# Attention split in three, first chunks laid out anew, W by a GpSimd sum and one exponential

The kernel runs on one core of a Trainium2 chip. The metric is device time in microseconds (us), less is better. All times are of executions of the whole program; span is the time from the first to the last instruction in the trace.

## The reference

An mLSTM cell feeds a feed-forward network (FFN) with squared relu; everything is fp32.

```python
# q, k, v, o_gate: (4, 8, 768, 40); i_gate, f_gate: (4, 8, 768); w_in (320, 2048); w_out (2048, 320)
for t in range(S):                                  # per batch and head
    m_new  = maximum(f[t] + m, i[t])
    f_stab = exp(f[t] + m - m_new);  i_stab = exp(i[t] - m_new);  m = m_new
    C = f_stab * C + i_stab * outer(v[t], k[t])
    n = f_stab * n + i_stab * k[t]
    y[t] = sigmoid(o[t]) * (C @ q[t]) / maximum(abs(n @ q[t]), 1)
x = y as (B*S, H*D) = (3072, 320)
out = maximum(x @ w_in, 0) ** 2 @ w_out             # weights arrive as float64 words
```

The kernel computes the cell in 24 chunks of 128 tokens (six for each batch). For a chunk, W is a masked matrix exp(A + b) of 128x1024 (8 heads of 128x128), the scores are weighted with it, and a state C is carried from chunk to chunk. The weights are rounded from float64 words in 26 pieces (10 of w_in, 16 of w_out) by ScalarE (`mag`, `low`) and VectorE (four instructions, `join`). All of w_out must be rounded by the time the second FFN matrix (FFN2) begins, near 122 us. What lies between the first FFN block and FFN2 is called the rounding stage below.

## The kernel before

`...` marks cuts.

```python
        def join(self):                       # rounding, VectorE's part of one piece
            ...                               # max/min, shift, and/xor on VectorE
            nc.vector.tensor_tensor(dst.bitcast(I32), bits, low.bitcast(I32), op=ALU.add)
            self.b.append(None)
            self.fetch()                      # the next weight piece's transfer

    def weigh(s):                             # W of chunk s
        ...
        if len(A) == 1:
            nc.gpsimd.affine_select(A[0][:], A[0][:], ...)      # the mask, 128x1024
        for i in range(len(A)):
            hh = slice(i * n, (i + 1) * n)
            for h in range(n):                                   # one exponential per head, b as bias
                nc.scalar.activation(d["W"][:, i * n + h, :], A[i][:, h, :], AF.Exp, bias=b_T[...])
            nc.scalar.activation(d["dec"][:, hh], A[i][:, :, P - 1], AF.Exp)
        values(s)

    def attend(s):
        # hi = qT * C (3 banks of pool ps_at in turn), dC = k * vw, hp = P * va, then on VectorE:
        # num = hi * eA;  Cn = dC * bdm;  and on GpSimd the update of C
        ...
    # half-steps u = 0..7 of the rounding stage
        else:                                  # u odd
            ...
            attend(s)
            rounding.step()
            normalise(s)                       # num += hp, dm, x_sb: VectorE
            ...
            transposes(s + 1)                  # kT by ScalarE, qT copied by VectorE (L356)
            ...
        while rounding.done < NEXT[u]:
            rounding.step()
```

## Time and profile before

| | before |
|---|---|
| time, median of 3 | 619.71 us (619.48 to 619.84) |
| span of the profiled run, mean granted clock | 618.4 us, 0.967 |
| first FFN block ends / FFN2 begins | 43.56 / 121.77 us |
| from there to the end | 496.6 us, TensorE without a wait but at the very end |
| TensorE at half clock | 10.7-17.5, 27.8-41.4, 68.7-75.6, 82.4-89.2, 109.7-116.5 us: 41.0 us |

The half-clock intervals are read from the clock column of narrow windows (0.50 or 0.51 in each of the five). A half-clock interval is counted as costing at most half its length (16 `hp` matmuls took 3.50 us in one against 1.92 us at full clock), so 41.0 us is 20.5 us of "lost clock", which is also span x (1 - mean granted clock). It is an upper bound, since idle time at half clock is counted too. The clock column has no record of the first 3.9 us. The table of windows of the kernel before, cut where the first FFN block ends and where FFN2 begins (columns: length, busy time of TensorE, its weight loads, VectorE, ScalarE, GpSimd, clock, share of the DMA engines, GB/s):

```profile
0.00:43.56 43.56, 35.93 (x205) 27.96 (x207) 30.25 (x64) 22.45 (x56) 9.83 (x20) 0.76 0.78 158
43.56:121.77 78.21, 66.48 (x414) 55.91 (x411) 58.36 (x127) 51.15 (x113) 9.98 (x11) 0.87 0.82 165
121.77:618.40 496.63, 493.24 (x2240) 310.53 (x2238) 144.42 (x294) 126.98 (x326) 47.80 (x56) 1.00 0.23 46
```

Everything to be won is in the first two rows: only there is TensorE idle, but for 3.4 us at the very end, and only there is the clock under 1.

### The profile page before, as it was taken

The numbers are of one execution on the slowest core, as the hardware profiler recorded it, in microseconds if no ns is written. First come the engines' busy times: TensorE is split into PE (matmuls) and PEld (weight loads), VectorE is DVE, ScalarE is ACT, GpSimd is POOL, SyncE is SP. The second block draws the span as 40 slices with busy tenths as digits, with TensorE's granted clock in tenths as the row PEclk, the third lists the DMA queues.
The fourth block names the chain that finished last, engine by engine and source line by source line (L and its number), as shares of the span: only waits on it lengthen the run. The fifth ranks groups of instructions, "written<-read, shape, count | busy, mean of one in ns | idle before, by whom it ended". The sixth has DMA issues, their size and how long they took to land.

```text
span 618.4 us, 7545 instructions
## 1 busy us (share of the span) xinstructions
PE 595.6 (96%) x2851; PEld 394.4 (64%) x2851; DVE 233.0 (38%) x485; ACT 200.6 (32%) x494; POOL 67.6 (11%) x87
## 2 busy tenths in 40 slices
PE   9688878999999999999999999999999999999997
PEld 6576757877655477745477754577754577743575
DVE  6858847743134341134331243421233441112200
ACT  4384657740514320214321514312214222012100
POOL 3211201021011110101110210000210120000000
PEclk8869779799999999999999999999999999999999
DMA  9927796993321332221331422031301000000000
GB/s 194 202 69 159 158 191 142 187 163 65 77 43 47 63 55 67 71 49 35 61 69 46 88 43 57 11 67 56 76 12 34 1 1 22 12 11 0 1 21 22
DMA packets 130901, 42.47 MB, mean 69 GB/s; under 512 B 101073, under 2 KB 127697, under 8 KB 130865
## 3 DMA queue, kind: packets, MB, share of 16 engines
q1 hardware_dynamic: 130768, 41.79, 33.5%
q8 instruction: 23, 0.38, 0.3%
q10 hardware_dynamic: 96, 0.20, 0.1%
q14 instruction: 14, 0.11, 0.1%
HBM read 37.95 MB, written 4.03 MB: 68 GB/s over the span
## 4 chain that ended last, share of the span: by engine, by line
PE 90%; ACT 4%; DVE 4%; DMA 1%; issue 1%; SPq 0%; DVEq 0%; ACTq 0%
PE o_ps L516 34%; PE h_ps L464 23%; PE h_ps L469 7%; PE hp L404 6%; PE tp L352 4%; PE h_ps L488 4%; PE tp L365 3%; PE hi L390 3%; PE dC L397 3%; PE tp L449 1%; DMA kq<-in_q_dram 1%; ACT W_sb L328 1%; PE A_ps L309 1%; PE h_ps L495 1%; PE A_ps L301 1%
## 5 line engine op out<-in xcount | busy, mean ns | idle before, releaser
L516 PE MATMUL o_ps<-w_out,g 128*128 128x320 f32 x768 | 213.8, 435 | 0.0
L516 PEld LDWEIGHTS o_ps<-w_out,g 128*128 128x128 f32 x768 | 143.5, 190 | 57.9 <-issue 0.8
L464 PE MATMUL h_ps<-xT,w_in 128*128 128x512 f32 x320 | 146.9, 602 | 0.0
L473 DVE TENSOR_TENSOR g<-r_sb 128x512 f32<-128x512 f32 x80 | 51.7, 688 | 148.0 <-ACT r_sb L472 148.0
L464 PEld LDWEIGHTS h_ps<-xT,w_in 128*128 128x128 f32 x320 | 57.7, 190 | 69.9 <-issue 65.2
L472 ACT ACTIVATE r_sb<-h_ps 128x512 f32<-128x512 f32 x80 | 43.5, 595 | 162.6 <-PE h_ps L469 162.5
L522 ACT COPY y_sb<-o_ps 128x320 f32<-128x320 f32 x24 | 10.2, 426 | 184.3 <-PE o_ps L516 184.3
L328 ACT ACTIVATE W_sb<-A_bc,b_T 128x128 f32<-128x128 f32 x176 | 53.7, 392 | 0.0
L379 DVE TENSOR_TENSOR P_sb<-tp,W_sb 128x512 f32<-128x512 f32 x46 | 29.6, 685 | 56.8 <-PE tp L365 45.4
L404 PE MATMUL hp<-va,P_sb 128*128 128x41 f32 x368 | 46.8, 290 | 0.0
L404 PEld LDWEIGHTS hp<-va,P_sb 128*128 128x128 f32 x368 | 45.6, 202 | 0.0
L469 PE MATMUL h_ps<-xT,w_in 64*128 64x512 f32 x160 | 45.2, 641 | 0.0
L356 DVE COPY qT<-tp 128x512 f32<-128x512 f32 x23 | 15.8, 688 | 73.5 <-PE tp L352 73.5
L339 POOL TENSOR_TENSOR vw<-va,W_sb 128x328 f32<-128x328 f32 x20 | 15.0, 751 | 258.7 <-ACT W_sb L328 244.9
L488 PE MATMUL h_ps<-xT,w_in 128*128 128x256 f32 x128 | 37.2, 453 | 5.0 <-ACT xT L450 4.6
L488 PEld LDWEIGHTS h_ps<-xT,w_in 128*128 128x128 f32 x128 | 29.0, 234 | 11.3 <-ACT xT L450 5.2
L423 POOL TENSOR_TENSOR C_sb<-C_sb,Cd 128x328 f32<-128x328 f32 x16 | 14.1, 880 | 163.1 <-DVE C_sb L415 163.1
L469 PEld LDWEIGHTS h_ps<-xT,w_in 64*128 64x128 f32 x160 | 12.0, 184 | 30.3 <-issue 30.3
L365 PEld LDWEIGHTS tp<-qT,kT 40*128 40x128 f32 x384 | 24.1, 187 | 10.1 <-issue 5.9
L352 PE MATMUL tp<-ident,kq 128*128 128x128 f32 x192 | 28.8, 299 | 1.7 <-DMA kq<-in_k_dram 1.2
L390 PEld LDWEIGHTS hi<-C_sb,qT 128*128 128x128 f32 x160 | 20.0, 191 | 12.9 <-issue 11.5
L365 PE MATMUL tp<-qT,kT 40*128 40x128 f32 x384 | 27.1, 280 | 0.9 <-DVE qT L356 0.9
(84 smaller groups left out, 442.6 us busy)
## 6 DMA issues: line engine op xcount, KB each, us to landing
A_bc<-a_rows SPq DMA_DIRECT2D x22, 512.0 KB, 3.9
raw<-in_moe_w_out_dram SPq DMA_DIRECT2D x16, 320.0 KB, 3.1
raw<-in_moe_w_in_dram SPq DMA_DIRECT2D x8, 512.0 KB, 4.8
kq<-in_k_dram SPq DMA_DIRECT2D x24, 160.0 KB, 3.8
kq<-in_q_dram SPq DMA_DIRECT2D x24, 160.0 KB, 4.5
va<-in_v_dram SPq DMA_DIRECT2D x24, 160.0 KB, 4.2
og<-in_o_gate_dram SPq DMA_DIRECT2D x24, 160.0 KB, 4.2
out_dram<-y_sb SPq DMA_DIRECT2D x24, 160.0 KB, 1.8
```

What stands on the lines that cost most here:

```text
L328: nc.scalar.activation(d["W"][:, i * n + h, :], A[i][:, h, :], AF.Exp, bias=b_T[:, b, c, i * n + h : i * n + h + 1],)
L352: nc.tensor.transpose(tp[:, j, :], d["kq"][:, i, 2 * j : 2 * j + 2, :].rearrange("p h d -> p (h d)"), ident[:],)
L365: nc.tensor.matmul(sc[i][:, j, :], lhsT=d["kT"][rows, j, :], rhs=d["qT"][rows, j, :], start=True, stop=True,)
L379: nc.vector.tensor_tensor(t, d["sc"][i], d["W"][:].rearrange("p (j two) t -> p j two t", two=2)[:, :, i, :], op=ALU.mult,)
L390: nc.tensor.matmul(hi[:, 2 * j : 2 * j + 2, :].rearrange("p h d -> p (h d)"), lhsT=d["qT"][:, j, :], rhs=C[:, j].rearrange("p h d -> p (h ...
L404: nc.tensor.matmul(hp[:, h, :], lhsT=d["P"][h % 2][:, h // 2, :], rhs=d["va"][:, h, :], start=True, stop=True,)
L464: nc.tensor.matmul(h[:], lhsT=w_in[:, a, fb * P : (fb + 1) * P], rhs=xT[:, a, :], start=(a == 0), stop=False,)
L469: nc.tensor.matmul(hs[i][:], lhsT=w_in2[rows, p, :], rhs=xT[rows, 2, :], start=False, stop=True)
L472: nc.scalar.activation(r[:], hs[i][:], AF.Relu)
L473: nc.vector.tensor_tensor(st["g2"][:, 2 * p + i, :], r[:], r[:], op=ALU.mult)
L488: nc.tensor.matmul(hs[i][:, n, :], lhsT=w_in[:, a, fb * P : (fb + 1) * P], rhs=xT[:, a, cols], start=(n == 0 and a == 0), stop=False,)
L516: nc.tensor.matmul(o_ps, lhsT=st["g2"][:, fb, j * P : (j + 1) * P], rhs=w_out[:, fb, :], start=(fb == 0), stop=(fb == NF - 1),)
```

## The change

The intent: take the eight exponentials of W off ScalarE (one sum on GpSimd, one exponential of 128x1024), take the last add of three weight pieces off VectorE, split the attention into `history`, `update` and `inside` so that the first two chunks can be laid out with fewer waits, load chunk 3 earlier, and lend PSUM banks otherwise. The diff, cut to its core:

```diff
-            nc.vector.tensor_tensor(dst.bitcast(I32), bits, low.bitcast(I32), op=ALU.add)
+            (nc.gpsimd if n < IN_DONE[0] else nc.vector).tensor_tensor(
+                dst.bitcast(I32), bits, low.bitcast(I32), op=ALU.add,
+            )
...
     def weigh(s):                        # chunks 2 to 23; chunks 0 and 1 keep eight (weigh_half)
+        nc.gpsimd.tensor_tensor(
+            d["W"][:], d["A"][:], b_T[:, b, c, :].unsqueeze(2).to_broadcast([P, H, P]), op=ALU.add,
+        )
+        nc.gpsimd.affine_select(d["W"][:], d["W"][:], ...)
-            for h in range(n):
-                nc.scalar.activation(d["W"][:, i * n + h, :], A[i][:, h, :], AF.Exp, bias=b_T[...])
+        nc.scalar.activation(d["dec"][:], d["A"][:, :, P - 1], AF.Exp)
+        nc.scalar.activation(d["W"][:], d["W"][:], AF.Exp)
...
+    def attend(s):
+        if s % NB:
+            history(s)                   # hi, and num right behind it on VectorE
+        if s % NB + 1 < NB:
+            update(s)                    # dC, Cn, C
+        inside(s)                        # hp
...
     # first chunks (after scores, W and weighted of chunks 0 and 1)
+    do_b(2, NB)                          # earlier: before, behind normalise(1)
+    scores(1)
+    weighted(1, spare=True)
+    turn_gates(2, NB)
     ...
+    update(0)
+    inside(0)
     ...
+    inside(1)
+    normalise(0)
+    history(1)
+    turn_rows(0)
+    normalise(1)
+    update(1)
+    idle(4)                              # bf16 matmuls on zeros, meant to keep the clock
     transposes(2)
+    rounding.join()
+    load_part(3, 0)
+    load_part(3, 1)
     ...
         else:                            # u odd
+            rounding.step()
             ...
             attend(s)
-            rounding.step()
             normalise(s)
```

More of the change, by code (lines that the diff above doesn't have):

```diff
@@ L252, in turn_gates @@
         for src, dst in ((i_sb, b_T), (A_sb, eA_T)):
-            tp = ps_o.tile([P, W], F32, name="tp", tag="o_ps")[:, : (c1 - c0) * BH]
+            tp = ps_h.tile([P, W], F32, name="tp", tag="h_ps") if c0 else ps_o.tile([P, W], F32, name="tp", tag="o_ps")
+            tp = tp[:, : (c1 - c0) * BH]
             tp = tp.rearrange("p (c r) -> p c r", r=BH)
@@ L292, in load_A @@
         A = ld.tile([P, H, P], F32, name="A_bc", bufs=2)
-        d["A"] = [A]
+        d["A"] = A
         nc.sync.dma_start(
@@ L296, in load_A, with mask_A @@
         )
-    def mask_A(s):
-        A = ps_h.tile([P, H // 2, P], F32, name="A_ps", tag="h_ps")
+    def mask_A(s, i):
+        pool, tag = (ps_at, "at") if s and i else (ps_h, "h_ps")
+        A = pool.tile([P, H // 2, P], F32, name="A_ps", tag=tag)
         nc.tensor.matmul(
@@ L312, in spread_A, with weigh_half @@
             )
+    def weigh_half(s, i):
+        b, c = divmod(s, NB)
+        d = st[s]
+        A, n = d["A"][i], H // 2
+        if i == 0:
+            d["W"] = prep.tile([P, H, P], F32, name="W_sb")
+            d["dec"] = prep.tile([P, H], F32, name="dec")
+        for h in range(n):
+            nc.scalar.activation(
+                d["W"][:, i * n + h, :], A[:, h, :], AF.Exp, bias=b_T[:, b, c, i * n + h : i * n + h + 1],
+            )
+        nc.scalar.activation(d["dec"][:, i * n : (i + 1) * n], A[:, :, P - 1], AF.Exp)
+        if i == 1:
+            values(s)
     def weigh(s):
@@ L316, in weigh @@
         d = st[s]
-        A, n = d["A"], H // len(d["A"])
         d["W"] = prep.tile([P, H, P], F32, name="W_sb")
-        d["dec"] = prep.tile([P, H], F32, name="dec")
-        if len(A) == 1:
-            nc.gpsimd.affine_select(
-                A[0][:], A[0][:], compare_op=ALU.is_ge, fill=-1e30, base=0, pattern=[[0, H], [1, P]], channel_multiplier=-1,
-            )
-        for i in range(len(A)):
-            hh = slice(i * n, (i + 1) * n)
-            for h in range(n):
-                nc.scalar.activation(
-                    d["W"][:, i * n + h, :], A[i][:, h, :], AF.Exp, bias=b_T[:, b, c, i * n + h : i * n + h + 1],
-                )
-            nc.scalar.activation(d["dec"][:, hh], A[i][:, :, P - 1], AF.Exp)
+        nc.gpsimd.tensor_tensor(
+            d["W"][:], d["A"][:], b_T[:, b, c, :].unsqueeze(2).to_broadcast([P, H, P]), op=ALU.add,
+        )
+        nc.gpsimd.affine_select(
+            d["W"][:], d["W"][:], compare_op=ALU.is_ge, fill=-1e30, base=0, pattern=[[0, H], [1, P]], channel_multiplier=-1,
+        )
+        d["dec"] = prep.tile([P, H], F32, name="dec")
+        nc.scalar.activation(d["dec"][:], d["A"][:, :, P - 1], AF.Exp)
+        nc.scalar.activation(d["W"][:], d["W"][:], AF.Exp)
         values(s)
@@ L381, in weighted, with history @@
             )
-    def attend(s):
+    def history(s):
+        d, C = st[s], st["C"]
         b, c = divmod(s, NB)
-        d = st[s]
-        C = st.get("C")
-        if c > 0:
-            hi = ps_at.tile([P, H, D1], F32, name="hi", tag="at")
-            for j in range(PR):
-                nc.tensor.matmul(
-                    hi[:, 2 * j : 2 * j + 2, :].rearrange("p h d -> p (h d)"), lhsT=d["qT"][:, j, :],
-                    rhs=C[:, j].rearrange("p h d -> p (h d)"), start=True, stop=True,
-                )
-        if c + 1 < NB:
-            dC = ps_at.tile([P, PR, 2, D1], F32, name="dC", tag="at")
-            for j in range(PR):
-                nc.tensor.matmul(
-                    dC[:, j].rearrange("p h d -> p (h d)"),
-                    lhsT=d["kq"][:, 0, 2 * j : 2 * j + 2, :].rearrange("p h d -> p (h d)"),
-                    rhs=d["vw"][:, 2 * j : 2 * j + 2, :].rearrange("p h d -> p (h d)"), start=True, stop=True,
-                )
+        d["hi"] = hi = ps_at.tile([P, H, D1], F32, name="hi", tag="at")
+        for j in range(PR):
+            nc.tensor.matmul(
+                hi[:, 2 * j : 2 * j + 2, :].rearrange("p h d -> p (h d)"), lhsT=d["qT"][:, j, :],
+                rhs=C[:, j].rearrange("p h d -> p (h d)"), start=True, stop=True,
+            )
+        num = d["num"] = work.tile([P, H, D1], F32, name="num")
+        nc.vector.tensor_tensor(
+            num[:], hi[:], eA_T[:, b, c, :].unsqueeze(2).to_broadcast([P, H, D1]), op=ALU.mult,
+        )
@@ new lines, in update @@
+    def update(s):
+        d, C = st[s], st.get("C")
+        dC = ps_at.tile([P, PR, 2, D1], F32, name="dC", tag="at")
+        for j in range(PR):
+            nc.tensor.matmul(
+                dC[:, j].rearrange("p h d -> p (h d)"),
+                lhsT=d["kq"][:, 0, 2 * j : 2 * j + 2, :].rearrange("p h d -> p (h d)"),
+                rhs=d["vw"][:, 2 * j : 2 * j + 2, :].rearrange("p h d -> p (h d)"), start=True, stop=True,
+            )
+        Cn = work.tile([P, PR, 2, D1], F32, name="C_sb")
+        nc.vector.tensor_tensor(Cn[:], dC[:], bdm[:], op=ALU.mult)
+        if s % NB:
+            Cd = work.tile([P, H, D1], F32, name="Cd")
+            nc.gpsimd.tensor_tensor(
+                Cd[:], C[:].rearrange("p j i d -> p (j i) d"),
+                d["dec"][:].unsqueeze(2).to_broadcast([P, H, D1]), op=ALU.mult,
+            )
+            Cf = Cn[:].rearrange("p j i d -> p (j i) d")
+            nc.gpsimd.tensor_tensor(Cf, Cf, Cd[:], op=ALU.add)
+        st["C"] = Cn
@@ L402, in attend, with inside @@
+    def inside(s):
+        d = st[s]
         hp = d["hp"] = ps_at.tile([P, H, D1], F32, name="hp", tag="at")
@@ L406, in attend @@
             )
-        d["num"] = hp
-        if c > 0:
-            num = d["num"] = work.tile([P, H, D1], F32, name="num")
-            nc.vector.tensor_tensor(
-                num[:], hi[:], eA_T[:, b, c, :].unsqueeze(2).to_broadcast([P, H, D1]), op=ALU.mult,
-            )
-        if c + 1 < NB:
-            Cn = work.tile([P, PR, 2, D1], F32, name="C_sb")
-            nc.vector.tensor_tensor(Cn[:], dC[:], bdm[:], op=ALU.mult)
-            if c > 0:
-                Cd = work.tile([P, H, D1], F32, name="Cd")
-                nc.gpsimd.tensor_tensor(
-                    Cd[:], C[:].rearrange("p j i d -> p (j i) d"),
-                    d["dec"][:].unsqueeze(2).to_broadcast([P, H, D1]), op=ALU.mult,
-                )
-                Cf = Cn[:].rearrange("p j i d -> p (j i) d")
-                nc.gpsimd.tensor_tensor(Cf, Cf, Cd[:], op=ALU.add)
-            st["C"] = Cn
+        d.setdefault("num", hp)
+    def attend(s):
+        if s % NB:
+            history(s)
+        if s % NB + 1 < NB:
+            update(s)
+        inside(s)
     def normalise(s):
@@ L570 @@
     make_consts()
+    load_part(1, 0)
+    load_part(1, 1)
     fetch(1)
-    for i in range(3):
-        load_part(1, i)
+    load_part(1, 2)
     fetch(1)
@@ L576 @@
     load_o(1)
-    fetch(2)
-    idle(7)
-    mask_A(0)
-    mask_A(0)
-    mask_A(1)
+    idle(4)
+    mask_A(0, 0)
+    mask_A(0, 1)
+    mask_A(1, 0)
     transposes(0)
+    mask_A(1, 1)
     do_gates(0, 2)
@@ L588 @@
     scores(0)
-    weigh(0)
+    spread_A(1, 0)
+    weigh_half(0, 0)
+    weigh_half(0, 1)
+    weigh_half(1, 0)
     do_gates(2, NB)
-    nc.scalar.dma_start(A_d[:, :], A_sb[:])
-    rounding.words()
-    spread_A(1, 0)
-    transposes(1, (False, True))
-    mask_A(1)
-    spread_A(1, 1)
-    weighted(0)
-    scores(1, (True, True))
-    weigh(1)
-    rounding.join()
-    load(2)
-    load_A(2)
-    attend(0)
-    weighted(1, spare=True)
-    rounding.words()
-    sigmoid(0)
-    sigmoid(1)
-    normalise(0)
-    load_o(2)
-    load_o(3)
-    rounding.join()
-    attend(1)
-    turn_rows(0)
-    normalise(1)
-    do_b(2, NB)
+    nc.sync.dma_start(A_d[:, :], A_sb[:])
+    fetch(2)
+    load_part(2, 0)
+    load_part(2, 1)
+    load_A(2)
+    load_part(2, 2)
+    weighted(0)
+    transposes(1, (True, True))
+    spread_A(1, 1)
+    weigh_half(1, 1)
+    do_b(2, NB)
+    scores(1)
+    weighted(1, spare=True)
     turn_gates(2, NB)
@@ L619 @@
     rounding.words()
+    update(0)
+    inside(0)
+    sigmoid(0)
+    sigmoid(1)
+    rounding.words()
+    rounding.join()
+    load_o(2)
+    load_o(3)
+    inside(1)
+    normalise(0)
+    st[1].pop("num")
+    history(1)
+    turn_rows(0)
+    normalise(1)
+    update(1)
+    idle(4)
     transposes(2)
+    rounding.join()
+    load_part(3, 0)
+    load_part(3, 1)
     turn_rows(1)
-    rounding.join()
+    rounding.step()
     weigh(2)
@@ L627 @@
     LOAD_A = (3,), (), (4,), (5,), (), (6,), (7,), (8,)
-    LOAD = (3,), (4,), (), (5,), (6,), (7,), (8,), (9,)
+    LOAD = (), (4,), (), (5,), (6,), (7,), (8,), (9,)
     LOAD_O = (), (), (4,), (5,), (6, 7), (), (8, 9), (10, 11)
@@ L631 @@
         s = 2 + u // 2
-        if u == 0:
-            ffn1_half(0, 0, 0)
-            scores(s)
-            rounding.step()
-            weighted(s)
-        elif u % 2 == 0:
-            scores(s)
-            turn_rows(s - 1)
-            ffn1_half(0, u // 4, u % 4)
+        if u % 2 == 0:
+            if u == 0:
+                ffn1_half(0, 0, 0)
+                scores(s)
+            else:
+                scores(s)
+                turn_rows(s - 1)
+                ffn1_half(0, u // 4, u % 4)
             rounding.step()
@@ L643 @@
         else:
+            rounding.step()
             if u in (1, 5):
@@ L647 @@
             attend(s)
-            rounding.step()
             normalise(s)
@@ L654 @@
                 ffn1_half(0, u // 4, u % 4)
+        for r in LOAD_A[u]:
+            load_A(r)
         while rounding.done < NEXT[u]:
             rounding.step()
+        if u == 0:
+            load_part(3, 2)
         square_half()
@@ L659 @@
             weigh(s + 1)
-        for r in LOAD_A[u]:
-            load_A(r)
         for r in LOAD[u]:
```

## The prediction

> **What bounds the kernel now.** First the busy table and the slices of the page.
>
> ```profile
> PE 595.6 (96%) x2851; PEld 394.4 (64%) x2851; DVE 233.0 (38%) x485; ACT 200.6 (32%) x494; POOL 67.6 (11%) x87
> ...
> PE   9688878999999999999999999999999999999997
> ...
> PEclk8869779799999999999999999999999999999999
> ```
>
> TensorE is the bound: 618.4 us less 595.6 busy leaves 22.8 us idle, nearly all in the first eight slices (to 124 us); the clock drops below 9 tenths only there. A mean granted clock of 0.967 means 0.033 x 618.4 = 20.4 us of lost clock time. So some 40 us is all that can be won, and only before 125 us; after that the queue of FFN matmuls never waits, and any us saved early comes off the end. Next, TensorE's waits (us in total, times, longest):
>
> ```profile
> PE hi L390 <- DVE P_sb L379: 5.2, 2, 2.7
> PE tp L256 <- DVE i_sb L249: 4.6, 1, 4.6
> PE h_ps L488 <- ACT xT L450: 4.6, 2, 3.6
> ...
> PE tp L352 <- DMA kq<-in_k_dram: 1.2, 1, 1.2
> ```
>
> The timeline shows what is behind the first and third: the eight exponentials of W.
>
> ```profile
> 62.08 1.28 ACT L328 ACT_TABLE_LOAD   x1
> ...
> 63.37 2.44 ACT L328 ACTIVATE W_sb<-A_bc,b_T 128x128 f32<-128x128 f32 x8
> 65.56 1.29 DVE L379 TENSOR_TENSOR P_sb<-tp,W_sb 128x512 f32<-128x512 f32 x2 [2.08 <-ACT W_sb L328]
> ...
> 66.39 1.09 PE L390 MATMUL hi<-C_sb,qT 128*128 128x82 f32 x8 [2.73 <-DVE P_sb L379]
> ```
>
> TensorE stops 2.73 us there for W of chunk 3, 3.62 us at 80.2 us for a row copy queued behind W of chunk 4 on ScalarE, 2.44 us at 106.3 us for W of chunk 5. Together 8.8 us. Last, GpSimd against VectorE:
>
> ```profile
> 27.86 1.10 POOL L322 TENSOR_SCALAR_AFFINE_SELECT A_bc<-A_bc 128x1024 f32<-128x1024 f32 x1
> 27.98 1.01 DVE L433 TENSOR_TENSOR dm<-dm,num 128x8 f32<-128x8 f32 x1
> ...
> 52.50 0.17 DVE L433 TENSOR_TENSOR dm<-dm,num 128x8 f32<-128x8 f32 x1
> ```
>
> The same tiny VectorE instruction takes 1.01 us while GpSimd works and 0.17 us otherwise.
>
> [...] in half-microsecond windows the clock falls or rises at 10.7, 17.5, 27.8, 41.4, 68.7, 75.5, 82.4, 89.2, 109.7 and 116.5 us[...]. [...]
>
> [...]
>
> [...] The trace has 751 ns for 328 elements[...].
>
> [...] The trace's 671 ns for 512 and 494 ns for 320 elements extend to 1.14 us.
>
> **The change part by part.**
>
> 1. W of chunks 2 to 23. ScalarE loses eight activations (2.44 us a chunk) and gains one of about 1.1 us: 1.3 us saved. GpSimd gains a sum of 1024[...], ahead of the select of 1.1 us that stays (1097 ns in the groups). From 125 us on a chunk takes some 22 us of TensorE time and GpSimd is 11% busy; sum and select end long before ScalarE asks, and the extra blocking of VectorE (33% busy) is hidden. Worth 0 there. Before 125 us it shortens the three waits: 3 x 1.3 = 3.9 us gained.
>
> 2. Loads of chunk 3. Its k and q were issued at 48.2 us, because they stood behind weight fetches that wait for buffers; TensorE waited 1.15, 0.52 and then 0.87 us for the copy of qT. Now they stand before most of those fetches. The copy's 0.7 us stays: 1.8 us gained.
>
> 3. The first two chunks. Before, the last gate transposes waited 4.6 us for two VectorE sums (L248, L249) queued behind the normalising of chunk 1; now the sums come right after qT of chunk 1 and their transposes before the attention products, so that wait goes. But scores of chunk 1 now take a bank in which the mask and gates of chunk 1's second half lay, so TensorE must wait for its four exponentials and `dec` (1.15 + 0.2 us, L328 and L331), some 1.4 us. [...] the clock should drop at 17.5 us, just before the small products of the attention. At half clock a product of 16 such instructions took 3.50 us (hp at 109.64) against 1.92. Two of these, two of dC and one of hi (1.1 us each, doubled on the weight loads) lose 2 x 1.6 + 3 x 0.65 = 5.2 us[...]. Then FFN would begin near 36 us as before, but wait for weight piece 1: VectorE gets to it only after qT of chunk 2, and its last add moves to GpSimd [...]. If the clock holds instead, FFN begins near 31 us. Before, the first FFN block ended at 43.5 us; with the drop I get 44.1, without it 37 to 38. I give the drop 6 in 10: 0.6 x (-0.6) + 0.4 x 6 = 2.0 us gained.
>
> 4. Lost clock. Of the three drops after 60 us each stretches what follows by about 3 us (16 L488 matmuls took 6.35 against 3.62 us after the wait at 83.85). With waits of about 1.3, 2.3 and 1.1 us, one of three should go, perhaps two: 3.5 us gained.
>
> 5. VectorE. Rounding three weight pieces moves 0.69 us each to GpSimd, outside the bottleneck. Against it, between 36 and 122 us VectorE is the second busiest engine (8.5, 7.3, 9.2 of 10 us from 50 to 80)[...]. A rounding step also now stands ahead of the attention's sums. [...]
>
> Sum: 3.9 + 1.8 + 2.0 + 3.5 - 3.1 = 8.1 us gained; 619.7 - 8.1 = 611.6.
>
> **The rivals.** (a) VectorE becomes the bound of the rounding stage. For it: 75% busy there already, strict order, GpSimd locks seen in the trace. Against: before it idled 2 to 3 us at each W wait. Worked through with every lock falling on it, qT of chunk 3 comes 3 us later, TensorE idles, a new clock drop follows, and the gain shrinks to about 2 us: 617.5. (b) The clock holds from 4 us through the prologue and two of the later drops go. [...] Then 6 more in part 3 and 3 in part 4: 602 to 604. (c) The first stage loses the clock already at 10.7 us [...]: the first FFN block ends near 48 us, 4.5 us later than now, and the other parts about pay for it: 616 to 621. (d) Later chunks: the exponential waits on GpSimd in ScalarE's queue and holds up the relus. With 20 us a chunk of slack I see no us in it.
>
> **Range and chances.** Between (a), near 617.5, and (b), near 603, with the sum at 611.6: 602.5 to 618.5. Faster by over 2% means under 607.3 us; only (b) or parts of it reach that: 0.27. Slower by over 2% (632) needs a new regular wait after 125 us, which I don't see: 0.02. The rest, 0.71.
>
> **What would show it.** After 130 us no wait of TensorE and an unchanged matmul rhythm (part 1); an exponential of 128x1024 at 1.0 to 1.2 us [...]; no DMA wait for k of chunk 3 (part 2); no wait at L256's successor, a wait of TensorE on ScalarE near 15 to 16 us and a clock drop at 17.5 us (part 3); at most two drops after 60 us (part 4); VectorE instructions of a microsecond or two beside the GpSimd sums (part 5). I'm wrong if the first FFN block doesn't end between 36 and 46 us, if the sum on GpSimd takes over 3 us, or if TensorE waits after 130 us.

The sum came to 8.1 us gained, 611.6 us. No trace here shows what makes the clock fall or rise; that a shorter wait keeps it (part 4) was the estimate. Measured in the kernel before: 751 ns is GpSimd's product `vw` (L339), 671 and 494 ns are ScalarE's `mag` (L179); "locks" stands for the 0.17 us that became 1.01 us beside a select; and 16 weight loads of `hp` took 1.87 us at full and 3.41 us at half clock.

## The result, and the profile after

| | before | after |
|---|---|---|
| time, median (fast runs) | 619.78 us (619.48 to 620.08, 4 runs) | 620.79 us (619.88 to 622.85, 4 runs) |
| span, clock of the profiled run | 618.4 us, 0.967 | 617.9 us, 0.967 |
| first FFN block ends / FFN2 begins | 43.56 / 121.77 us | 44.57 / 121.88 us |
| half clock | 41.0 us | 11.8-35.7, 49.3-56.2, 83.5-86.9, 110.8-117.6 us: 41.0 us |

The ratio is 1.0021, with a 95% interval of 0.9996 to 1.0046: the same time. A ratio here is the mean time of one kernel's fast runs over that of the other's of the same rounds, so it is not quite the ratio of the medians. The predicted 611.6 us (602.5 to 618.5) is missed on the slow side.

The page of the changed kernel, to be read beside the same lines of before in the prediction:

```profile
PE 598.3 (97%) x2851; PEld 397.2 (64%) x2852; DVE 261.5 (42%) x482; ACT 170.5 (28%) x340; POOL 114.7 (19%) x112
...
PEclk8587989799999999999999999999999999999999
```

ScalarE lost 30.1 us of work, GpSimd gained 47.1 and VectorE 28.5, though three adds had left VectorE. These 28.5 us are not new work but instructions that last longer. The windows, cut at the same two events:

```profile
0.00:44.57 44.57, 40.55 (x205) 32.74 (x208) 28.91 (x60) 18.22 (x44) 12.78 (x21) 0.73 0.79 152
44.57:121.88 77.31, 65.03 (x413) 53.76 (x411) 65.95 (x129) 50.19 (x97) 20.72 (x19) 0.89 0.81 172
121.88:617.90 496.02, 492.70 (x2240) 310.72 (x2238) 166.64 (x294) 102.06 (x200) 81.16 (x73) 1.00 0.23 45
```

The last row: VectorE holds 22 us more there and GpSimd 33 us more, and the stage is not slower (496.0 against 496.6 us). The second row is where the change should have paid. VectorE went from 58.4 of 78.2 us (75%) to 66.0 of 77.3 us (85%), TensorE idles 12.3 us against 11.7, and nothing is won. TensorE's waits of the changed kernel (us in total, times, longest):

```profile
PE tp L367 <- DVE num L409: 5.2, 2, 3.5
PE hi L404 <- ACT xT L476: 2.3, 2, 1.4
PE h_ps L514 <- ACT xT L476: 2.0, 2, 1.4
PE h_ps L514 <- POOL w_in L199: 1.7, 1, 1.7
PE dC L418 <- POOL vw L354: 1.6, 1, 1.6
```

The waits for W (2.7, 3.6 and 2.4 us before) have shrunk to 1.4, 1.4 and 0.9 us at the same places, and that for the transfer of chunk 3 has gone. In their place come waits on `num`: the transposes of the next chunk take the PSUM bank of `hi`, which comes free only when VectorE has read it for `num`. The timeline of VectorE and TensorE shows why that is late (start, length, engine and line):

```profile
107.12 0.32 DVE L190 TENSOR_SCALAR mag<-mag 128x320 f32<-128x320 f32 x1
...
110.22 0.49 DVE L199 CUSTOM_DVE_ANT_0 w_out<-mag,low 128x640 uint16<-128x640 uint16 x1
110.62 0.32 DVE L190 TENSOR_SCALAR mag<-mag 128x320 f32<-128x320 f32 x1
...
111.97 0.49 DVE L199 CUSTOM_DVE_ANT_0 w_out<-mag,low 128x640 uint16<-128x640 uint16 x1
112.38 0.49 DVE L409 TENSOR_TENSOR num<-hi,eA_T 128x328 f32<-128x328 f32 x1
```

```profile
112.93 1.11 PE L367 MATMUL tp<-ident,kq 128*128 128x128 f32 x4 [3.45 <-DVE num L409]
```

`hi` was done at about 107.1 us. Three weight pieces of 1.75 us each stood ahead of `num`; the change had put the third there (the step before `attend`); two stood ahead of `num` at this place in the kernel before, too. The wait of 1.6 us on `vw` is another matter: it is W of chunk 2, whose sum, select and exponential now stand in one chain before the product dC (GpSimd, ScalarE, TensorE):

```profile
42.60 2.07 POOL L337 TENSOR_TENSOR W_sb<-A_bc,b_T 128x1024 f32<-128x1024 f32 x1
...
46.20 1.06 ACT L346 ACTIVATE W_sb<-W_sb 128x1024 f32<-128x1024 f32 x1 [3.22 <-POOL W_sb L341]
...
48.14 1.12 PE L418 MATMUL dC<-vw,kq 128*128 128x82 f32 x8 [1.63 <-POOL vw L354]
```

The clock drops at 49.3 us, right behind this wait; there was no drop here before. And this is what the GpSimd sum does to VectorE:

```profile
55.23 1.90 POOL L337 TENSOR_TENSOR W_sb<-A_bc,b_T 128x1024 f32<-128x1024 f32 x1
55.34 1.82 DVE L459 TENSOR_TENSOR dm<-dm,num 128x8 f32<-128x8 f32 x1
...
57.20 1.09 POOL L341 TENSOR_SCALAR_AFFINE_SELECT W_sb<-W_sb 128x1024 f32<-128x1024 f32 x1
57.31 1.32 DVE L464 TENSOR_TENSOR x_sb<-num,og 128x320 f32<-128x320 f32 x1
```

A VectorE instruction on 8 columns lasts 1.82 us, as long as the sum beside it. Before it was 0.17 us without GpSimd and 1.01 us beside a select. The groups of the whole run give the mean lengths of the new operations:

```profile
L337 POOL TENSOR_TENSOR W_sb<-A_bc,b_T 128x1024 f32<-128x1024 f32 x22 | 42.3, 1924 | 4.3 <-DMA A_bc<-a_rows 4.3
...
L346 ACT ACTIVATE W_sb<-W_sb 128x1024 f32<-128x1024 f32 x22 | 23.1, 1049 | 3.2 <-POOL W_sb L341 3.2
```

### The profile page after: what moved, and what is told of

Its sections match the earlier page's. It is cut to its first block, busy times and chain, and to the rows that moved or that the text cites. A ratio compares the mean times of both kernels' runs of the same rounds, so it can differ in the third digit from the quotient of the medians.

```text
span 617.9 us, 7395 instructions
## 1 busy us (share of the span) xinstructions
PE 598.3 (97%) x2851; PEld 397.2 (64%) x2852; DVE 261.5 (42%) x482; ACT 170.5 (28%) x340; POOL 114.7 (19%) x112
## 4 chain that ended last, share of the span: by engine, by line
PE 91%; ACT 3%; DVE 3%; issue 1%; POOL 1%; DMA 1%; SPq 1%; DVEq 0%; POOLq 0%; ACTq 0%
PE o_ps L542 34%; PE h_ps L490 23%; PE h_ps L495 7%; PE hp L440 7%; PE tp L367 4%; PE tp L380 3%; PE h_ps L514 3%; PE dC L418 3%; PE hi L404 3%; PE tp L475 1%; PE A_ps L313 1%; PE A_ps L305 1%; PE h_ps L521 1%; DVE mag L195 1%; ACT r_sb L533 1%
## 5 line engine op out<-in xcount | busy, mean ns | idle before, releaser
L490 PEld LDWEIGHTS h_ps<-xT,w_in 128*128 128x128 f32 x320 | 57.7, 190 | 69.9 <-issue 65.2
L548 ACT COPY y_sb<-o_ps 128x320 f32<-128x320 f32 x24 | 10.2, 425 | 185.8 <-PE o_ps L542 185.8
L337 POOL TENSOR_TENSOR W_sb<-A_bc,b_T 128x1024 f32<-128x1024 f32 x22 | 42.3, 1924 | 4.3 <-DMA A_bc<-a_rows 4.3
L514 PE MATMUL h_ps<-xT,w_in 128*128 128x256 f32 x128 | 35.2, 432 | 4.0 <-ACT xT L476 2.0
L514 PEld LDWEIGHTS h_ps<-xT,w_in 128*128 128x128 f32 x128 | 27.3, 221 | 9.8 <-POOL w_in L199 2.1
L367 PE MATMUL tp<-ident,kq 128*128 128x128 f32 x192 | 26.9, 285 | 5.2 <-DVE num L409 5.2
L367 PEld LDWEIGHTS tp<-ident,kq 128*128 128x128 f32 x192 | 23.1, 148 | 7.2 <-DVE num L409 5.6
```

The costliest lines, as they stand in the source:

```text
L337: nc.gpsimd.tensor_tensor(d["W"][:], d["A"][:], b_T[:, b, c, :].unsqueeze(2).to_broadcast([P, H, P]), op=ALU.add,)
L367: nc.tensor.transpose(tp[:, j, :], d["kq"][:, i, 2 * j : 2 * j + 2, :].rearrange("p h d -> p (h d)"), ident[:],)
L490: nc.tensor.matmul(h[:], lhsT=w_in[:, a, fb * P : (fb + 1) * P], rhs=xT[:, a, :], start=(a == 0), stop=False,)
L514: nc.tensor.matmul(hs[i][:, n, :], lhsT=w_in[:, a, fb * P : (fb + 1) * P], rhs=xT[:, a, cols], start=(n == 0 and a == 0), stop=False,)
```

## The experiments

Three theories of why the gain was given back, in the order in which some expectations number them (T1, T2, T3):

- Order: the rounding step now stands ahead of `num` on VectorE and keeps PSUM banks from TensorE.
- Load: VectorE, with its instructions held up by the GpSimd sum, sets the pace of the rounding stage.
- Clock: the new layout of the first chunks loses the clock from 11.8 to 35.7 us, and that eats what the layout saves.

18 kernels were run. All gave correct results. Every ratio is to the kernel before, of the same rounds; "stage" is from the end of the first FFN block to the begin of FFN2 in the profiled run.

### The step back behind attend

```diff
 # changed kernel, u odd
-            rounding.step()
             ...
             attend(s)
+            rounding.step()
             normalise(s)
```

> The changed kernel with one line moved back: in the odd half-steps of the rounding stage the weight rounding step stands after the attention's sums again, as in the kernel before. Theory T1 (the order on VectorE: the sum over hi comes late, its PSUM bank isn't freed, and TensorE waits for it 3.45 us at 109.5 us and 1.79 us at 72.9 us): both waits of the chunk transposes on num vanish or fall under 1 us in all, and the clock drop at 110.6 us goes; 620.8 becomes 612 to 616. Rival T2 (the locks of GpSimd's longer work hold VectorE up, whatever its order): the lateness only moves to another instruction; 619 to 621.

618.26 us (616.45 to 621.53), ratio 0.9964 (0.9907 to 1.0022). The stage shrank from 77.3 to 71.6 us, but it began at 47.83 (after: 44.57), because the clock dropped once more from 39.7 to 46.5 us. That is not the edit's doing, which lies behind it: three more runs with edits behind the first stage (old W, no step, step and qT) have the same drop and begin the stage at 47.8 to 48.1. The stage lost 5.1 us of clock against 8.5. TensorE's waits of this run, from 30 us on:

```profile
PE tp L380 <- DVE qT L371: 3.2, 1, 3.2
PE tp L380 <- ACT g L535: 2.1, 1, 2.1
...
PE tp L367 <- DVE num L409: 1.7, 1, 1.7
```

The wait on `num` fell from 5.2 to 1.7 us, as the order theory said. A new one of 3.2 us came: the rounding step now stands where the sum on GpSimd is expected, and one of its instructions (L195) lasted 2.27 and twice 2.07 us in place of 0.69 and 0.49; the copy of qT stands behind it. The interval includes 1, so this alone settles nothing.

### The old W in the new order

```diff
 # changed kernel, weigh(s)
-        nc.gpsimd.tensor_tensor(d["W"][:], d["A"][:], b_T[...], op=ALU.add)
-        nc.gpsimd.affine_select(d["W"][:], d["W"][:], ...)
+        nc.gpsimd.affine_select(d["A"][:], d["A"][:], ...)
+        for h in range(H):
+            nc.scalar.activation(d["W"][:, h, :], d["A"][:, h, :], AF.Exp, bias=b_T[:, b, c, h : h + 1])
-        nc.scalar.activation(d["W"][:], d["W"][:], AF.Exp)
```

> The changed kernel with W of the later chunks as before: select on GpSimd in place, eight exponentials with pointer bias on ScalarE, no sum on GpSimd. T2 (locks): VectorE instructions of 1.8 to 2.3 us beside the sums vanish, VectorE gains some 2 us a chunk, and the time falls by 2 to 5 us to 616 to 619. T1 (order): VectorE's locks matter little, ScalarE loses 1.3 us a chunk, W is late again and the time rises by 2 to 5 us, to 623 to 626.

624.54 us (624.29 to 625.32), ratio 1.0062 (1.0013 to 1.011). VectorE's busy time in the rounding stage fell from 66.0 to 57.3 us, and still the run was slower, with waits of 4.3 us on xT and 2.6 us on P_sb behind the eight exponentials, and 58.0 us at half clock. But TensorE idled less in the stage than in the changed kernel (10.6 against 12.3 us), and the fast runs lost 28.3 us of clock against 23.1, more than the 3.8 us by which they are slower. So this run doesn't weigh VectorE's load against the 1.3 us more of ScalarE in each chunk: the clock covers the difference.

### The three adds back on VectorE

```diff
-            (nc.gpsimd if n < IN_DONE[0] else nc.vector).tensor_tensor(
+            nc.vector.tensor_tensor(
```

> The changed kernel with the last add of the first three weight pieces on VectorE again. The first FFN block waited 1.67 us for the GpSimd add of piece 1 (1.31 us there against 0.69 us on VectorE), and W of chunk 2 stands behind the add of piece 2 in GpSimd's queue. If these matter: the FFN wait falls to about 1 us, W of chunk 2 comes 1 to 2.5 us earlier and the wait of dC on vw (1.63 us) goes; the time falls by 1 to 3 us. If the VectorE queue is what is scarce there: no change within 1 us.

621.10 us (619.9 to 623.43), ratio 1.001 (0.9948 to 1.0073). The first FFN matmuls waited 1.9 us for VectorE's add in place of 1.7 us for GpSimd's. These runs show no difference by where the three adds run.

### The kernel before with the new W alone

```diff
 # kernel before, weigh(s), chunks 2 to 23
+            nc.gpsimd.tensor_tensor(d["W"][:], A[0][:], b_T[...], op=ALU.add)
+            nc.gpsimd.affine_select(d["W"][:], d["W"][:], ...)
+            nc.scalar.activation(d["dec"][:], A[0][:, :, P - 1], AF.Exp)
+            nc.scalar.activation(d["W"][:], d["W"][:], AF.Exp)
-            (select in place and the eight exponentials)
```

> The kernel before with only the W of later chunks changed (GpSimd sum, select, one exponential). If part 1 of the prediction holds alone: the three waits behind W (2.73, 3.62, 2.44 us) shrink by about 1.3 us each, 3.9 us in all, perhaps with a clock drop less (another 3 us): 613 to 617. If GpSimd's locks on VectorE take it back (T2): 618 to 622.

622.81 us (618.23 to 623.27), ratio 1.0015 (0.9956 to 1.0074). In the kernel before too the new W gains nothing: VectorE's busy time in the stage went from 58.4 to 65.2 us, and new waits came on `num` (3.9), `dec` (2.4) and qT (2.0 us).

### Idle matmuls in the first stage ("warm")

```diff
 # changed kernel; idle(n): n bf16 matmuls of 128x512 on zeros
     weigh_half(1, 0)
+    idle(3)
...
     transposes(1, (True, True))
+    idle(3)
     spread_A(1, 1)
     weigh_half(1, 1)
+    idle(3)
...
     update(0)
+    idle(2)
     inside(0)
+    idle(3)
...
     inside(1)
+    idle(3)
```

> The changed kernel with 17 more idle matmuls (0.21 us each at full clock, 3.6 us in all) spread over the first stage, to keep the clock through it. In the changed kernel it ran at half from 11.8 to 35.7 us. Theory T3 (the clock lost in the first stage ate what the new order should have won): the clock holds from 4 us [...], FFN begins at 30 to 34 us instead of 37.9 and the time falls by 3 to 6 us. Rival T4 (VectorE and ScalarE set the pace there): the clock holds but FFN begins no earlier than 36 us; within 2 us of the changed kernel.

615.68 us (614.40 to 617.66), ratio 0.9936 (0.9911 to 0.9961). The first FFN matmul began at 33.48 us (37.88 after), FFN2 at 117.94 (121.88). Its clock by slices:

```profile
PEclk8978989899999999999999999999999999999999
```

17 instructions that compute nothing win 5 us: the first stage's clock does cost the changed kernel time. Half clock fell from 41.0 to 30.7 us. Where the gain appears is less plain: the first FFN block ended at 43.12 us, only 1.5 us earlier (44.57), after a wait of 1.7 us for weight piece 1 and a drop from 35.0 to 41.8 us; the rounding stage took 74.8 us (77.3) with as much lost clock (8.5 us).

### No step ahead of attend at all

```diff
 # changed kernel, u odd
-            rounding.step()
```

> The changed kernel with the weight rounding step of the odd half-steps taken behind the normalising and the copy of qT, where the loop over the remaining steps makes it up. The run with the step between attend and normalise had only moved the wait: to qT (3.2, 2.1 and 1.2 us). T1 (order): no wait of the chunk transposes on num and none of the scores on qT over 1 us, and 612 to 616. T2 (locks): the normalising itself is locked out by the sums (1.8 us and 1.3 us instructions), qT still late by 2 us twice, and 617 to 620.

623.85 us (622.95 to 624.79), ratio 1.0066 (1.0051 to 1.0081). The catch-up loop does the step later. The waits on `num` went, but others came, of this run from 30 us on:

```profile
PE h_ps L514 <- ACT xT L476: 5.0, 2, 4.3
PE h_ps L514 <- ACT r_sb L533: 3.3, 1, 3.3
```

ScalarE idled up to 5.8 us because its next `mag` waits for a buffer that VectorE frees when it joins a piece, and row copies and relus stand behind that `mag` in ScalarE's order. So the order theory in its plain form ("take the step away from `num`") is wrong: a late step costs more than an early one.

### The sum done twice

```diff
 # changed kernel, weigh(s): the sum into W, done a second time ahead of the select
+        nc.gpsimd.tensor_tensor(d["W"][:], d["A"][:], b_T[...], op=ALU.add)
```

> The changed kernel with the GpSimd sum of every later chunk made twice (the same result). T2 (locks set the pace of the rounding stage): VectorE loses up to 1.9 us more a chunk there and W of chunk 2 comes 2 us later; the time rises by 3 to 8 us. T1 (order alone): 0 to 2 us. After 125 us no wait of TensorE in either, if part 1's claim that these stages hide it holds.

630.36 us (628.13 to 632.11), ratio 1.0169 (1.0144 to 1.0193), 9.6 us over the changed kernel. The windows say where:

```profile
46.89:134.30 87.41, 70.95 (x413) 57.87 (x411) 71.64 (x128) 50.14 (x97) 28.97 (x23) 0.84 0.71 150
134.30:630.30 496.00, 492.70 (x2240) 310.72 (x2238) 188.75 (x294) 102.79 (x200) 115.84 (x90) 1.00 0.23 45
```

The stage grew from 77.3 to 87.4 us; behind FFN2's begin it stayed at 496.0 us with 34.7 us more of GpSimd. The four sums of the stage are 7.6 us of GpSimd time, and their second run costs 10.1 us there: 5.2 us are lost clock (13.7 against 8.5 us), and TensorE idles 4.2 us longer. So the sum does lie on the path before FFN2, and nowhere else. The run doesn't tell whether it does so through VectorE's held-up instructions or as a part of the way to W.

### Warm, no step ahead of attend, and weight piece 1 joined earlier

```diff
 # warm version
+    rounding.join()
     history(1)
...
     transposes(2)
-    rounding.join()
... u odd
-            rounding.step()
```

> The idle matmuls of e4, the order of e5, and the join of weight piece 1 ahead of the history sum of chunk 1 (VectorE idled 3.5 us there), so that the FFN's wait for piece 1 (1.67 us) goes. If the three causes add up: 606 to 611. If one limit takes over from the other: 613 to 617.

621.31 us over all four runs (619.5 to 622.41 for the three fast ones, one slow at 633.44), ratio 1.0015 (0.9992 to 1.0037). The first FFN block ended at 38.47 us, 6 us earlier than after, and FFN2 still began at 124.41: with the rounding steps late, FFN2 begins when it did without the warm first stage (124.52), after a stage of 85.9 us, 15.4 us of it lost clock (76.7 and 8.5 us in the run without warmth). What is won in the first stage is lost again here.

### Warm, and weight piece 1 joined earlier

```diff
 # warm version
+    rounding.join()
     history(1)
...
     transposes(2)
-    rounding.join()
```

> The warm version (17 idle matmuls) with the join of piece 1 (its last add on GpSimd) moved ahead of the first chunk's history, step order of the changed kernel kept. The wait of 1.67 us for GpSimd at the first FFN matmuls goes and with it the drop of the clock that followed it (35.0 to 41.8), so the first FFN block should end near 38.5 in place of 43.1. If TensorE alone sets the pace behind it, all of this 4.6 us reaches the end: 611 us. If VectorE with its held-up instructions sets the pace of the rounding stage, FFN2 begins near 117 to 119 all the same and the time is 615 to 617, within 1.5 us of the warm version. I expect the second.

615.35, 615.85, 618.21, 619.52 us and, slow, 627.43; ratio of the fast 0.9929 (0.9869 to 0.999). The range is the finding. The profiled run is the slow one, at half clock from 12.5 to 43.2 us; the fast ones had granted clocks of 0.970 to 0.978, the slow one 0.959. It is the same as the warm version within its spread; the early join is worth nothing that can be seen.

### The same with the step behind attend

```diff
 # version above, u odd
-            rounding.step()
             attend(s)
+            rounding.step()
             normalise(s)
```

> The same as the warm version with the early join, and the odd half-steps' rounding step back where the kernel before had it, between attend and normalise. If the place of the step ahead of num is a large part of what was lost, the wait of transposes on num (3.5 and 1.8 us) shrinks and the stage to FFN2 takes 73 to 76 us: 612 to 614 us, faster than before by 1 per cent. If the holds simply fall on another instruction ahead of qT and kT (as in the run that moved the step alone), 616 to 618 us.

611.28 and 615.82 us fast, 624.29 and 627.05 us slow; ratio of the two fast ones 0.9882 (0.9798 to 0.9967), unclear. The mean granted clocks were 0.986, 0.981, 0.964 and 0.959, in the order of the times. One program gives 611 or 627 us. The only trace is of a slow run (half clock from 12.1 to 42.8 us); the fast ones have none, so that the first stage's clock makes the difference is likely and not shown.

### Control: idle matmuls in the kernel before

```diff
 # kernel before
     spread_A(1, 1)
+    idle(3)
     weighted(0)
     scores(1, (True, True))
+    idle(3)
...
     attend(0)
+    idle(3)
...
     turn_rows(0)
+    idle(16)
```

> Control: the kernel before with idle matmuls only (3 after the second half of A of chunk 1 is spread, 3 after scores(1), 3 after attend(0), 16 after turn_rows(0), where TensorE waits 4.6 us for VectorE). If the time won by the warm version is the clock's alone and needs nothing of the change, the half-clock time of the first 45 us (20.4 us before) falls to 7 or less, FFN2 begins 5 to 7 us earlier, and the time is 613 to 615 us. If the change's split of attention is needed for it (the gain comes of the order), it stays at 618 to 620 us.

621.06 us (619.85 to 628.57), ratio 1.0029 (0.9953 to 1.0105). Half clock in the first 45 us fell from 20.4 to 10.2 us, and the first FFN block ended at 43.81 us, as before (43.56). The gates' transposes came at 33.0 us, still on VectorE's sums (L249; a wait of 1.14 us, 4.6 before). So in the kernel before, as this profile reads, VectorE's sums set the end of the first stage more than the clock does. That the gain of the warm version needs the change's layout fits this; the idle matmuls stood at other places, so it is not proved.

### Control: the early load of chunk 3 in the kernel before

```diff
 # kernel before
     load_o(3)
+    load(3)
-    LOAD = (3,), (4,), (), (5,), (6,), (7,), (8,), (9,)
+    LOAD = (), (4,), (), (5,), (6,), (7,), (8,), (9,)
```

> The kernel before with the loads of chunk 3 alone issued right after the o gate's second load, which is part 2 of the change alone. The prediction put it at 1.8 us gained of the 2.5 us of waits for a transfer of chunk 3. If so, those waits are gone and the time is 617.5 to 619; if they were hidden by VectorE's pace of the rounding stage, 619 to 620.5, with the waits turned into waits on VectorE.

619.22 us (618.41 to 623.93), ratio 0.9975 (0.9917 to 1.0033): the median is 0.2 us outside the first expectation and inside the second; the interval holds both. The waits for the transfer went in the profiled run, the one on the copy of qT grew from 0.9 to 1.7 us.

### qT of chunks 3 to 5 copied by ScalarE

```diff
 # transposes(s): in the changed kernel, in the warm version, and in the kernel before
-            (nc.scalar.copy if i == 0 or s == 0 else nc.vector.tensor_copy)(d[n][:], tp)
+            (nc.scalar.copy if i == 0 or s in (0, 3, 4, 5) else nc.vector.tensor_copy)(d[n][:], tp)
```

In the changed kernel:

> The changed kernel with the copies of qT of chunks 3, 4 and 5 on ScalarE in place of VectorE: 3 x 0.69 us leave VectorE's queue before FFN2, and qT no longer stands behind held-up instructions; ScalarE has 8 exponentials less per chunk than the kernel before and 27 us free in this stage. If VectorE's pace and its held-up instructions are what gave the gain back, the stage from the first FFN block to FFN2 shortens by 2 to 4 us (77.3 to 74 or 75) and the time is 617 to 618.5 us at the same lost clock. If the clock alone decides, the stage is unchanged and the time stays at 620 to 622.

620.65 us (619.01 to 623.43), ratio 0.9995 (0.9952 to 1.0039). VectorE had 1.9 us less in the stage, and nothing was won; the stage took 80.2 us in the profiled run, at a clock of 0.83 (0.89 after). Waits from 30 us on:

```profile
PE tp L367 <- DVE num L409: 3.9, 2, 2.1
PE h_ps L514 <- ACT xT L476: 2.9, 2, 2.2
```

In the warm version:

> The warm version with the same move of qT. Its wait of 3.4 us on qT goes. If VectorE sets the pace of the stage behind a warm start, FFN2 begins 2 to 3 us sooner (117.9 to 115 or 116) and the time is 612.5 to 614 us, beating both kernels by about 1 per cent. If not, 615 to 617.5 as the warm version.

616.46 us (614.77 to 618.9), ratio 0.9927 (0.9885 to 0.997): as the warm version, no more. The wait of 3.5 us on `num` stayed.

In the kernel before, as a control:

> Control: the kernel before with the same move. There ScalarE still has the eight exponentials of W ahead of row copies and relus, and it is ScalarE that TensorE waits for. If VectorE's queue is the limit of the changed kernel only, nothing is gained here: 619 to 622 us. If VectorE bounds the rounding stage in both kernels alike, the kernel before gains 1.5 to 3 us too: 617 to 618.5.

614.97 us (614.43 to 619.82), ratio 0.9931 (0.9881 to 0.9981). This missed: the control gained where the changed kernel did not. Its stage took 73.7 us (78.2 before), and its mean lost clock over five runs was 18.1 us. Less load on VectorE went with a gain in the kernel before, in which `num` stands ahead of the step, and with none in the changed one. The two intervals overlap, and the lost clock fell along with the time, so this speaks against load as such and does not refute it.

### Both edits at once: step behind attend and qT on ScalarE

The edits are the ones shown above, on the changed kernel:

> The changed kernel with two edits at once: the odd half-steps' rounding step back between attend and normalise, and the copies of qT of chunks 3 to 5 on ScalarE. Each alone left a wait of the other kind (the step alone 3.2 us on qT behind held-up VectorE instructions, the copy alone 3.9 us on num behind the step). If the gain is given back by where a held-up VectorE instruction stands ahead of something TensorE needs, both together remove both waits: stage to FFN2 of 70 to 74 us, 614 to 617 us at a lost clock of about 20 us. If the clock alone or VectorE's sheer load decides, 618 to 621 us.

615.63 us (614.69 to 617.5), ratio 0.9897 (0.9836 to 0.9958). TensorE's waits from 30 us on:

```profile
PE tp L380 <- ACT qT L371: 3.9, 1, 3.9
...
PE tp L367 <- DVE num L409: 0.4, 1, 0.4
```

The wait on `num` is down to 0.4 us, the stage takes 70.5 us (77.3 after), at a mean clock of 0.95 there (0.89). The interval lies wholly under the changed kernel's (0.9996 to 1.0046); it overlaps with that of the step alone, whose stage took 71.6 us, so that the copy is needed as well is not shown. Of the 6.8 us that the stage is shorter, lost clock is 5.1 (8.5, then 3.4 us), and TensorE idles 2.7 us less (the two overlap in part). In ratio to before, the step alone moved the changed kernel by -0.0057, the copy alone by -0.0026, both by -0.0124. It isn't that all waits went: qT now waits 3.9 us for ScalarE, once.

And on the warm version:

> The warm version with the same two edits. If order and warmth add up, FFN2 begins at 113 to 116 us and the time is 609 to 613 us, faster than every other version; if not, 614 to 617.

610.43 us, all five runs between 610.10 and 610.73; ratio 0.9811 (0.9759 to 0.9863), so whether it is faster by 2% is unclear, but that it beats both kernels is not: its slowest run is 7.8 us under the fastest of the kernel before in the same rounds. From the changed kernel's 1.0021, warmth alone gave -0.0085 and the two edits alone -0.0124; together -0.0210: they add up. The clock by slices and the two stages:

```profile
PEclk9998999999999999999999999999999999999999
```

```profile
0.00:39.40 39.40, 34.95 (x220) 25.75 (x225) 29.56 (x60) 18.36 (x44) 13.06 (x21) 0.96 0.89 174
39.40:112.42 73.02, 62.41 (x413) 52.43 (x411) 64.98 (x126) 51.16 (x100) 21.63 (x19) 0.93 0.81 179
```

VectorE is as busy as in the changed kernel (65.0 against 66.0 us in the stage), and TensorE's waits between the first FFN block and FFN2 are 10.6 us in all against 12.3. The half clock is down from 41.0 to 13.6 us: 13.7 us less lost clock, where the span is 9.4 us shorter. Most of the gain is clock.

The last control, the kernel before with qT on ScalarE and the early load:

> The kernel before with qT of chunks 3 to 5 on ScalarE (which alone gave about 0.7 per cent) and the early load of chunk 3. The 1.5 and 0.5 us of waits for chunk 3's transfer, which that run still showed, go: 612 to 615 us if they reach the end, 614.5 to 617 if another wait takes their place.

623.99 us (619.49 to 624.55), ratio 1.0017 (0.9959 to 1.0076). The waits for the transfer went, and the time rose over the same kernel without the early load: 9 us by the medians, which are of two chips, 5.3 us by the ratios. Its granted clocks were 0.953 in four of five runs and 0.967 in the fastest; the version without the early load had 0.967 to 0.972.

### All runs side by side

Median is of all runs, the ratio of fast runs; lost clock is span x (1 - mean granted clock), the mean of the fast runs; FFN2 is its begin in the profiled run (* slow).

| kernel | median us | ratio | lost clock us | FFN2 us |
|---|---|---|---|---|
| changed | 620.79 | 1.0021 | 23.1 | 121.9 |
| step behind attend | 618.26 | 0.9964 | 21.0 | 119.5 |
| old W | 624.54 | 1.0062 | 28.3 | 126.7 |
| adds on VectorE | 621.10 | 1.0010 | 23.9 | 123.3 |
| no step | 623.85 | 1.0066 | 23.5 | 124.5 |
| sum twice | 630.36 | 1.0169 | 28.1 | 134.3 |
| qT on ScalarE | 620.65 | 0.9995 | 22.9 | 124.8 |
| step and qT | 615.63 | 0.9897 | 17.9 | 118.6 |
| warm | 615.68 | 0.9936 | 11.8 | 117.9 |
| warm, early join | 618.21 | 0.9929 | 14.8 | 129.4* |
| warm, qT | 616.46 | 0.9927 | 14.1 | 120.9 |
| warm, step and qT | 610.43 | 0.9811 | 9.6 | 112.4 |
| warm, early join, no step | 621.31 | 1.0015 | 15.9 | 124.4 |
| warm, early join, step behind | 620.06 | 0.9882 | 10.1 | 129.0* |
| before, new W | 622.81 | 1.0015 | 23.3 | 125.2 |
| before, warm | 621.06 | 1.0029 | 18.5 | 122.1 |
| before, early load | 619.22 | 0.9975 | 20.7 | 125.5 |
| before, qT on ScalarE | 614.97 | 0.9931 | 18.1 | 116.0 |
| before, qT and early load | 623.99 | 1.0017 | 27.5 | 121.1 |

The kernel before itself, in nine runs: spans of 616.8 to 618.3 us in the five with 19 to 21 us of lost clock, 622.2 to 625.8 us in the four with 27 to 33 us. An edit that removes a wait of 2 us is judged on this ground: runs of one kernel lie 4 us and more apart, along with their lost clock.

## Why the prediction was wrong

The prediction was a sum of five terms, 8.1 us gained; the profile gave 0.5 us of span and the runs none. Term by term, each measured on the two profiles:

| term | predicted | measured | how |
|---|---|---|---|
| 1, W | +3.9 | about +5.2 | waits of 8.8 us became 1.39 + 1.36 + 0.86 |
| 2, loads | +1.8 | about +1.7 | 2.5 us became 0.87 |
| 3, first stage | +2.0 | -1.0 | first FFN block ends 44.57, not 43.56 |
| 4, clock after 60 us | +3.5 | at most +1.7 | half clock behind the first block 20.5, then 17.1 us |
| 5, VectorE | -3.1 | about -7.5 | 5.2 on `num`, 0.6 on `r_sb`; the 1.6 on `vw` is W of chunk 2 on GpSimd, so part 1's |

The measured terms overlap (half clock is counted over waits too: TensorE is busy in 4.67 of the 6.8 us from 110.8 to 117.6 us), so their sum of about 0 is a check and not a proof. One reading of the prediction was off by little, and nothing hangs on it: after 125 us VectorE is 30% busy and GpSimd 10% (143.9 and 47.6 of 475 us), not 33% and 11%.

Parts 1 and 2 were right in mechanism and near in size for the waits that they named. Part 1 missed one: W of chunk 2, whose sum lies on the path (1.6 us). The sum took 1.92 us (over 3 us was to show the prediction wrong), the exponential 1.05 us (1.1), there is no wait of TensorE after 130 us and the last 496 us are unchanged.

Part 3's drop branch came, and was bigger. I had the clock held until 17.5 us, then lost; it was lost at 11.8 already and came back at 35.7, which was rival (c). TensorE was busy without a gap from 4.0 to 11.5 us, before the drop, and in 23.64 of the 23.9 us at half clock; why the clock fell is not shown. The block's end at 44.57 is near the 44.1 of the drop branch. The wait of scores(1) for a lent bank, 1.4 us, did not happen. The +2.0 us came from 4 chances in 10 of 6 us for a clock that holds, so this term is the second step that failed, by 3.0 us. That the clock costs time here is shown: idle matmuls alone bring the first FFN matmul from 37.88 to 33.48 us and 0.85 points of time, though only 1.5 us of it at the end of the first FFN block. The control on the kernel before gained nothing, which fits a gain that needs the change's layout.

Part 4 said that shorter waits would let one of three drops go. That came: the drop at 68.7 us went, the next became half as long, and only two are left after 60 us. But a new one came at 49.3 us, behind the wait for W of chunk 2.

Part 5 is the step that failed most, with 3.1 us lost. It counted the sum's duration and took a share of it, an estimate. What it left out is order. I had written that a rounding step now stood ahead of the attention's sums, and gave it no time. That step is 1.75 us of VectorE in front of `num`, `num` holds the PSUM bank of `hi`, and TensorE's transposes of the next chunk need that bank: two waits of 1.8 and 3.5 us, 5.2 us in all. The step itself accounts for 2 x 1.75 = 3.5 us of them; the 1.7 us left stand behind the two pieces that were ahead of `num` before the change too, and 1.7 us is what the run with the step moved back still shows.

Of the rivals, (c) with 616 to 621 us holds the measured time; the stated range, drawn between (a) and (b), left its upper part out. Its number was partly luck: its first FFN block was to end near 48 us and ended at 44.57. Rival (a), "VectorE becomes the bound of the rounding stage", with 617.5 us, was 3 us off. In its plain form it is not supported: 1.9 us less VectorE (qT) changed nothing, and the run with 8.7 us less (old W) lost too much clock to tell. What the runs support is this: the change's rounding stage gives back its gain where VectorE's order puts rounding and held-up instructions ahead of `num` and ahead of qT. Moving the step alone brought a wait of 3.2 us on qT, moving the copy alone left 3.9 us on `num`; moving both gains 1.2 points over the changed kernel. How much of this is the waits and how much the clock (8.5, then 3.4 us lost in the stage) is not separated.

What stays open: how much of a single edit's effect is its own wait and how much the clock, which came out at 19 to 33 us lost in nine runs of the kernel before; what makes it drop is not shown. The qT copy gave 0.7% on the kernel before, and adding an early load took it all away along with the clock (18.1 to 27.5 us lost). I can't say why the warm version with step and qT regains its clock in five runs of five and the one with the early join and the step behind in two of four. And the doubled sum's 9.6 us are not divided between VectorE's held-up instructions and the way to W.

## What to carry to other kernels

When a change removes a wait, ask what stands in line right behind it on each engine, and which PSUM bank or buffer that instruction frees: here a step of 1.75 us, twice ahead of `num`, was 3.5 us of the 5.2 that TensorE waited for it. Work moved to GpSimd was not free for VectorE; beside a 1.9 us sum a VectorE instruction of 0.17 us took 1.82 us. And where the clock is at stake, look at the granted clock of every run before reading a difference of a per cent: here one program took 611.28 us at a granted clock of 0.986 and 627.05 (a slow run) at 0.959, and the best version has both the idle matmuls (-0.0085 in ratio alone) and the two edits to VectorE's order and load (-0.0124 alone).
